# Loading one more half expert by whole rows, with smaller column slabs at the end

## The chip, the cores and the metric

The kernel runs on one core of a Trainium2 chip. The metric is the time of one execution on the device in microseconds (us), the median of several runs. A profile's span, from the program's first to its last instruction, is some 1.8 us shorter than that time (176.1 us in the profiled run of the kernel before, whose time was 177.85).

## The reference

Attention with a sliding or dilated window over 8 x 8 heads of 576 tokens makes 4608 token rows of 512. A soft mixture of experts then works on them: 8 experts, 4 slots each.

```python
logits = x @ phi                                   # 4608 x 32
slot_input = softmax_over_tokens(logits).T @ x     # 32 slots, 4 for each expert
for e in range(8):
    h = np.maximum(slot_input[e] @ w1[e], 0.0)     # w1: 8 x 512 x 1024 float32
    slot_out[e] = h @ w2[e]                        # w2: 8 x 1024 x 512 float32
return softmax_over_slots(logits) @ slot_out       # 4608 x 512 float32 out
```

w1 and w2 are 2 MB each for an expert, 32 MB in all, and the output is 9.44 MB.

## The kernel before

The loads go through GpSimd's DMA queue, which converts float32 to bf16 on the way (half an expert, 1 MB of float32, lands as 512 KB in the issue table); only phi and one piece of w1 come through SyncE's queue. The order of the loads is fixed. Attention's inputs and w1 come first, then w2 expert by expert. Experts 0 to 5 are loaded by whole rows. Experts 6 and 7 come last and are cut into two column halves, the "slabs": columns 0 to 255 of both, then columns 256 to 511 of both. When the first slab is there, the first half of the output's columns can be computed and stored while the second slab is still loading.

```python
def w2_piece(e, c0=0, n=8):          # whole rows
    ... moe_w2[e].rearrange("(p c) f -> p (c f)", c=8)[:, c0 * DM:(c0 + n) * DM]
    return (fn, n << 18, f"w2_{e}{c0}", b_w2[e] if e < 5 else [b_w5h[c0 // 4]])

def w2_slab(e, s, c0=0, n=8):        # 256 columns of each row: runs of 1 KB
    ... moe_w2[e].rearrange("(p c) f -> p c f", c=8)[:, c0:c0 + n, 256 * s:256 * s + 256]

wq += [w2_piece(e) for e in range(5)] + [w2_piece(5, 0, 4), w2_piece(5, 4, 4)]
for s in range(2):
    wq += [w2_slab(6, s), w2_slab(7, s, 0, 4), w2_slab(7, s, 4, 2),
           w2_slab(7, s, 6, 1), w2_slab(7, s, 7, 1)]
# ...
l2((0, 1, 2, 3), 0, 0, 512)          # L857: matmuls of the second layer, whole width
l2((4,), 0, 0, 512)
for y in range(2):
    l2((5,), 0, 0, 512, range(4 * y, 4 * y + 4), [b_w5h[y]])
# L872, L875: ScalarE and VectorE empty this accumulator
for x in (1, 2):                     # the two column halves
    l2((6,), x, 256 * x - 256, 256, bufs=[b_w2[6][x - 1]])
    for y, cs in enumerate((range(4), range(4, 6), range(6, 7), range(7, 8))):
        l2((7,), x, 256 * x - 256, 256, cs, [b_w2h[y][x - 1]])
    # L881: VectorE adds this half to the sum
# ... L901 output matmul, L910/L913 its eviction, L922 store
NA = 2.5                             # groups of 512 tokens stored in two column halves
```

With NA = 2.5 there are five first-half stores of 256 KB, five second-half stores of 256 KB, and then whole-width stores. A small list scheduler fixes each engine's order of instructions when the program is built.

The softmax here doesn't subtract the row's maximum and nothing guards it: scores larger than these inputs give would overflow.

Of the kernel before, what the change touches and what calls it, by code (L numbers as in the profile page):

```python
# [54 lines left out]
class Sched:  # L55
# [8 lines left out]
    def op(self, eng, fn, dur, prio, reads=(), writes=(), rmw=(), after=(), banks=(), name="",  # L64
           kind="c", nbytes=0, rate=422e3, lag=0.0, sem=None, tail=False):
        o = Op()
        o.eng, o.fn, o.dur, o.prio, o.name = eng, fn, dur, prio, name
        o.kind, o.bytes, o.rate, o.lag, o.sem, o.tail = kind, nbytes, rate, lag, sem, tail
        o.deps, o.succ = set(), []
        o.banks, o.opens, o.ord = [], [], None  # L70
        o.seq = len(self.ops)
        for a in after:
            if a is not None:
                o.deps.add(a)
        for b in reads:
            o.deps.update(b.w)
            b.r.append(o)
        for b in writes:
            if b.r:
                b.prev = b.w + b.r  # L80
                b.w, b.r = [], []
            o.deps.update(b.prev)
            b.w.append(o)
        for b in rmw:
            o.deps.update(b.prev)
            o.deps.update(b.w)
            o.deps.update(b.r)
            b.w.append(o)
        for b in list(reads) + list(writes) + list(rmw) + list(banks):
            if isinstance(b, Bank) and b not in o.banks:  # L90
                o.banks.append(b)
                if b.left == 0:
                    o.opens.append(b)
                b.left += 1
        o.deps.discard(o)
        self.ops.append(o)
        return o
# [99 lines left out]
def bass_dilated_sliding_attn__then__soft_moe_slots_kernel(  # L197
# [60 lines left out]
    def a(off, dims, p0=0, pn=128):  # L258
        return AP(ar, p0 * NBF + off, [[NBF, pn]] + dims)
# [4 lines left out]
    def af(off, dims, p0=0, pn=128):  # L264
        return AP(ar_f.tensor, (p0 * NBF + off) // 2, [[NBF // 2, pn]] + dims)
# [4 lines left out]
    def pf(bank, off, dims, p0=0, pn=128):  # L270
        return AP(ps, p0 * 4096 + bank * 512 + off, [[4096, pn]] + dims)
# [10 lines left out]
    def pet(n, cols):  # L282
        return (40.0 + n * max(cols / 2.4, 27.0)) * PE_SLOW / 1000.0
# [4 lines left out]
    def dvet(n, psum=False):  # L288
        return ((120 if psum else 58) + n) / 960.0
# [16 lines left out]
    b_w1 = [Buf(f"w1{e}") for e in range(8)]  # L306
    b_w2 = [[Buf(f"w2{e}{s}") for s in range(2)] for e in range(8)]
    b_sx = Buf("sx")
    b_w5h = [Buf(f"w5h{x}") for x in range(2)]
    b_w2h = [[Buf(f"w2h{x}{s}") for s in range(2)] for x in range(4)]  # L310
    b_htz, b_rt, b_so = Buf("htz"), Buf("rt"), [Buf("soA"), Buf("soB")]
    b_hsb = [Buf(f"hsb{x}") for x in range(2)]
# [1 line left out]
    def w2off(e):  # L314
        return o_w2 + e * 8 * DM if e < 5 else o_stg + (e - 5) * 8 * DM
# [25 lines left out]
    wq = []  # L341
# [15 lines left out]
    def w1_piece(e, r0=0):  # L357
        def fn():
            return pool.dma_start(a(o_w1 + e * 4096 + 1024 * r0, [[1, 4096 - 1024 * r0]]),
                                  w1_rows(e)[:, 1024 * r0:])  # L360
        return (fn, (4 - r0) << 19, f"w1_{e}", [b_w1[e]])

    def w2_piece(e, c0=0, n=8):
        def fn():
            return pool.dma_start(
                a(w2off(e) + c0 * DM, [[1, n * DM]]),
                moe_w2[e].rearrange("(p c) f -> p (c f)", c=8)[:, c0 * DM:(c0 + n) * DM])
        return (fn, n << 18, f"w2_{e}{c0}", b_w2[e] if e < 5 else [b_w5h[c0 // 4]])

    def w2_slab(e, s, c0=0, n=8):  # L370
        def fn():
            return pool.dma_start(  # L372
                a(w2off(e) + 256 * s + c0 * DM, [[DM, n], [1, 256]]),
                moe_w2[e].rearrange("(p c) f -> p c f", c=8)[:, c0:c0 + n, 256 * s:256 * s + 256])
        return (fn, n << 17, f"w2s_{e}{s}{c0}", [b_w2[e][s] if n == 8 else b_w2h[(0, 4, 6, 7).index(c0)][s]])

    wq += [w1_piece(e, 2 if e == 0 else 0) for e in range(8)]
    wq += [w2_piece(e) for e in range(5)] + [w2_piece(5, 0, 4), w2_piece(5, 4, 4)]
    for s in range(2):
        wq += [w2_slab(6, s), w2_slab(7, s, 0, 4), w2_slab(7, s, 4, 2),  # L380
               w2_slab(7, s, 6, 1), w2_slab(7, s, 7, 1)]
    nw = [0]

# [467 lines left out]
    def l2(es, x, col, n, cs=range(8), bufs=None):  # L851
        def fn():
            last = None
            for c in cs:
                for e in es:
                    g, j = e // 4, e % 4
                    last = pe.matmul(pf(sobank[x].idx, 0, [[1, n]], 32 * j, 32),  # L857
                                     a(o_htz + 1024 * g + 128 * c + 32 * j, [[1, 32]]),
                                     a(w2off(e) + DM * c + col, [[1, n]]),
                                     start=(c == 0 and (g == 0 or x > 0)),  # L860
                                     stop=(c == 7 and (x > 0 or e in (2, 3, 4, 5))))
            return last

        op(PE, fn, pet(len(cs), n * .92), T1 + 5 + 2 * es[0] + (20 if x == 2 else 0) + cs[0] / 8,
           reads=[b_htz] + (bufs or [b_w2[e][y] for e in es for y in range(2)]),
           rmw=[sobank[x]], name=f"L2{es[0]}{x}{cs[0]}")

    l2((0, 1, 2, 3), 0, 0, 512)
    l2((4,), 0, 0, 512)
    for y in range(2):  # L870
        l2((5,), 0, 0, 512, range(4 * y, 4 * y + 4), [b_w5h[y]])
    op(ACT, lambda: act.activation(a(o_so, [[1, 512]], 0, 64), pf(sobank[0].idx, 0, [[1, 512]], 0, 64),  # L872
                                   ACTF.Copy), actt(512), T1 + 10, reads=[sobank[0]], writes=b_so,
       name="SOx")
    op(DVE, lambda: dve.tensor_copy(af(o_sx, [[1, 512]], 64, 64), pf(sobank[0].idx, 0, [[1, 512]], 64, 64)),  # L875
       dvet(512, True), T1 + 10, reads=[sobank[0]], writes=[b_sx, b_p[2]], name="SOy")
    for x in (1, 2):
        l2((6,), x, 256 * x - 256, 256, bufs=[b_w2[6][x - 1]])
        for y, cs in enumerate((range(4), range(4, 6), range(6, 7), range(7, 8))):
            l2((7,), x, 256 * x - 256, 256, cs, [b_w2h[y][x - 1]])  # L880
        op(DVE, lambda x=x: dve.tensor_tensor(  # L881
            a(o_so + 256 * x - 256, [[1, 256]], 64, 64), pf(sobank[x].idx, 0, [[1, 256]], 64, 64),
            af(o_sx + 512 * x - 512, [[1, 256]], 64, 64), AluOp.add), dvet(256, True),
           T1 + 10 + 20 * x, reads=[sobank[x], b_sx], writes=[b_so[x - 1]], name=f"SO{x - 1}")
# [69 lines left out]
    for o in order:  # L954
        c = o.sem if o.kind == "dma" else ctr[o.eng]
# [4 lines left out]
        for d in o.deps:  # L960
            if d.eng == o.eng == PE:
                continue
            s, val = d.ev
# [60 lines left out]
```

## Time and profile before

| | before |
|---|---|
| median of 3 runs | 177.89 us |
| span of the profile | 176.1 us |
| MB written by DMA | 41.26 |
| last weight piece landed | 152.19 us into the span |
| first output store issued | 148.57 us |
| last store landed | 175.61 us |

Landings are read from the trace's record of DMA completions. From the last weight landing to the last store's landing is 23.42 us; I call it the tail. The prediction shows the lines of this profile.

In these lines PE is TensorE and PEld its weight loads, DVE is VectorE, ACT is ScalarE, POOL is GpSimd, and SP is SyncE, which issues the stores. `ar` and `ps` are the program's names for on-chip data and for accumulators, and L857 is line 857 of the kernel. A line of the windows table gives a stretch of time and its length, the busy time and number of instructions of PE, PEld, DVE, ACT and POOL, the granted TensorE clock as a share of full speed, the DMA share, and the GB/s written. The DMA share is the time of all packets over the time of 16 engines. Here it passes 1 (1.45 with the slabs), so the times of some packets overlap.

### The profile page before, as it was taken

What the parts mean: (1) busy time and instruction counts of PE and PEld (TensorE: products, weight loads), DVE (VectorE), ACT (ScalarE), POOL (GpSimd) and SP (SyncE); (2) the same over time, 40 slices, a digit from 0 to 9 for tenths busy, and PEclk for the clock granted to TensorE, in tenths of its full rate; (3) what the DMA queues carried; (4) which work ended last, traced back from release to release, by engine and by line L of the source; (5) the groups of instructions that cost most, each with busy time, mean ns of one, the idle gap of its engine ahead of it and who ended that gap; (6) DMA issues with size and microseconds to landing.
All of it is one profiled execution on the core that took longest, in us unless ns stands there. A gap on an engine that the chain in (4) does not pass through costs nothing.

```text
span 176.1 us, 4787 instructions
## 1 busy us (share of the span) xinstructions
PE 129.5 (74%) x2102; PEld 86.8 (49%) x2102; DVE 120.5 (68%) x218; ACT 104.4 (59%) x165; POOL 44.9 (25%) x90
## 2 busy tenths in 40 slices
PE   0008786799698998999998989996779676797000
PEld 0005564567566776676777567765434334431000
DVE  6899395669998989989998999657220014399200
ACT  2404378568879969889889788884301113299000
POOL 7659622214142223311460000394000000000000
PEclk9999999789999999999999999999755999999955
DMA  5999999999999999999999999999999999999997
GB/s 186 233 210 210 224 201 210 227 201 209 220 210 208 219 214 208 214 217 205 216 215 204 209 216 221 220 212 216 216 220 203 204 195 196 296 312 415 422 419 318
DMA packets 17492, 41.26 MB, mean 234 GB/s; under 512 B 1728, under 2 KB 8384, under 8 KB 15040
## 3 DMA queue, kind: packets, MB, share of 16 engines
q0 software_dynamic: 13328, 30.41, 90.2%
q1 hardware_dynamic: 4144, 10.55, 15.7%
q8 instruction: 16, 0.26, 0.5%
q14 instruction: 4, 0.03, 0.0%
HBM read 61.93 MB, written 9.44 MB: 405 GB/s over the span
## 4 chain that ended last, share of the span: by engine, by line
DMA 32%; PE 23%; DVE 21%; ACT 10%; POOL 4%; issue 2%; POOLq 0%; DVEq 0%
DMA ar<-in_moe_w_dram 18%; DMA ar<-in_v_dram 14%; PE ps L509 6%; DVE ar L488 6%; DVE ar L913 6%; ACT ar L548 5%; POOL ar L372 3%; PE ps L603 3%; PE ps L570 3%; ACT ar L670 2%; PE ps L693 2%; DVE ar L614 2%; PE ps L516 2%; PE ps L526 2%; ACT ar L576 2%
## 5 line engine op out<-in xcount | busy, mean ns | idle before, releaser
L548 ACT ACTIVATE ar<-ps 128x1152 bf16<-128x1152 f32 (+1 forms) x32 | 38.0, 1186 | 22.8 <-PE ps L533 13.2
L488 DVE STREAM_TRANSPOSE ar<-ar 128x576 uint32<-128x576 uint32 x40 | 48.3, 1239 | 0.6 <-DMA ar<-in_k_dram 0.3
L509 PE MATMUL ps<-ar 128*128 128x320 bf16 (+1 forms) x128 | 23.8, 312 | 15.5 <-DVE ar L488 13.7
L614 DVE TENSOR_TENSOR ar<-ps,fs 96x768 bf16<-96x768 f32 (+1 forms) x32 | 26.3, 822 | 1.2
L576 ACT ACTIVATE ar<-ps 128x768 bf16<-128x768 bf16 x32 | 25.0, 812 | 1.1 <-PE ps L570 1.0
L509 PEld LDWEIGHTS ps<-ar 128*128 128x128 bf16 x128 | 10.8, 102 | 21.0 <-DVE ar L488 13.7
L603 PE MATMUL ps<-ar 128*128 128x65 bf16 x320 | 15.6, 199 | 4.2 <-ACT ar L548 4.2
L570 PE MATMUL ps<-ar 128*128 128x128 bf16 x192 | 15.9, 229 | 1.8 <-DVE ar L614 1.0
L603 PEld LDWEIGHTS ps<-ar 128*128 128x128 bf16 x320 | 12.8, 101 | 7.4 <-ACT ar L548 4.8
L910 ACT ACTIVATE ar<-ps,fs 128x512 f32<-128x512 f32 (+1 forms) x23 | 11.4, 638 | 7.6 <-PE ps L901 7.6
L335 POOL DMA_DIRECT2D ar<-in_k_dram x16 | 8.9, 553 | 27.5 <-DVE ar L488 26.7
L610 DVE RECIPROCAL fs<-ps 96x12 f32<-96x12 f32 (+1 forms) x32 | 6.6, 206 | 12.7 <-PE ps L603 12.2
L570 PEld LDWEIGHTS ps<-ar 128*128 128x128 bf16 x192 | 12.4, 118 | 2.9 <-DVE ar L614 1.2
L913 DVE TENSOR_SCALAR ar<-ps,fs 128x512 f32<-128x512 f32 (+1 forms) x23 | 12.7, 629 | 1.0 <-PE ps L901 1.0
L335 POOL DMA_DIRECT2D ar<-in_v_dram x16 | 8.8, 547 | 13.7 <-DVE ar L488 10.4
L857 PE MATMUL ps<-ar 128*32 128x512 bf16 (+1 forms) x80 | 9.6, 338 | 2.9 <-DMA ar<-in_moe_w_dram 1.4
L693 PE MATMUL ps<-ar 128*128 128x288 bf16 x64 | 10.2, 307 | 1.2 <-ACT ar L677 1.2
L335 POOL DMA_DIRECT2D ar<-in_q_dram x16 | 8.7, 545 | 8.8 <-DVE fs L610 5.3
L901 PE MATMUL ps<-ar 128*128 128x512 bf16 (+1 forms) x46 | 9.9, 340 | 1.3 <-DVE ar L881 1.0
L670 ACT ACTIVATE ar<-ps 128x576 bf16<-128x576 bf16 x16 | 9.7, 659 | 0.9 <-PE ps L654 0.7
L673 ACT ACTIVATE ar<-ps 128x1024 bf16<-128x1024 bf16 x8 | 8.2, 1030 | 2.5 <-PE ps L660 2.3
L494 DVE STREAM_TRANSPOSE ar<-ar 128x160 uint32<-128x160 uint32 (+1 forms) x32 | 9.5, 409 | 0.1
(75 smaller groups left out, 182.8 us busy)
## 6 DMA issues: line engine op xcount, KB each, us to landing
ar<-in_moe_w_dram POOLq DMA_DIRECT2D x12, 1024.0 KB, 25.9
out_dram<-ar SPq DMA_DIRECT2D x6, 1024.0 KB, 8.6
ar<-in_k_dram POOLq DMA_DIRECT2D x16, 288.0 KB, 21.1
ar<-in_q_dram POOLq DMA_DIRECT2D x16, 288.0 KB, 21.5
ar<-in_v_dram POOLq DMA_DIRECT2D x16, 288.0 KB, 20.5
ar<-in_moe_w_dram POOLq DMA_DIRECT2D x5, 512.0 KB, 28.1
out_dram<-ar SPq DMA_DIRECT2D x10, 256.0 KB, 3.8
ar<-in_moe_w_dram SPq DMA_DIRECT2D x1, 1024.0 KB, 5.1
```

Source lines behind the costliest of these rows:

```text
L335: return pool.dma_start(a(o_stg + (s * 3 + j) * 1152, [[1, 1152]]), src[b, 4 * dl:4 * dl + 4].rearrange("h (p t) d -> (h p) (t d)", p=32))
L488: return dve.transpose(au(o_dst, [[1, 18], [18, 32]]), au(src, [[32, 18], [1, 32]]))
L509: pe.matmul(pf(h, 0, [[1, W]]), a(o_id, [[1, 128]]), a(msk, [[1, W]]), start=True, stop=False)
L548: eo = op(ACT, lambda P=P, W=W: act.activation(a(P, [[W, 4], [1, W]]), AP(ps, 0, [[4096, 128], [512, 4], [1, W]]), ACTF.Exp, scale=SCALE), ...
L570: last = pe.transpose(pb(bank.idx, bb * 256 + par * 32, [[64, 4], [1, 32]]), src, a(o_id, [[1, 128]]))
L576: op(ACT, lambda t=t, bank=bank: act.activation(a(o_vb[vs] + 3 * t * VBK, [[66, 12], [2, 32], [1, 2]]), pb(bank.idx, 0, [[64, 12], [1, 32] ...
L603: last = pe.matmul(pf(bank.idx + x, 65 * t, [[1, 65]]), w, a(VB + t * VBK + 66 * h, [[1, 65]]), start=True, stop=True)
L614: op(DVE, lambda hp=hp, bank=bank: dve.tensor_tensor(a(ox + 128 * hp, [[64, 2], [256, NT], [1, 64]], 0, rows), pf(bank.idx, 0, [[512, 2], ...
L670: fn = lambda c=c + x, bank=bank: act.activation(a(o_xt[xt] + 576 * c, [[1, 576]]), pb(bank.idx, 0, [[1, 576]]), ACTF.Copy)
L693: last = pe.matmul(pf(bank.idx, 0, [[1, 288]]), a(o_phis + 128 * c, [[1, 128]]), a(o_xt[xt] + 576 * c + 288 * g, [[1, 288]]), start=(c == ...
L910: op(ACT, lambda: act.activation(dst, src(), ACTF.Copy, scale=sca), actt(cw, .1), prio + .1, reads=[bank, b_rinv], writes=wr, name=f"OE{G} ...
L913: op(DVE, lambda: dve.tensor_scalar(dst, src(), sca, None, op0=AluOp.mult), dvet(cw, True) + .08, prio + .1, reads=[bank, b_rinv], writes= ...
```

## The change

The intent is to move bytes out of the slow slabs and into fast whole rows (196 against 216 GB/s written in the profile before), without losing the overlap of the second slab with the first-half stores. Half of expert 6's rows are loaded whole and go into the whole-width accumulator. The slabs shrink from 4 MB to 3 MB in all, and expert 5 comes in one transfer.

```diff
-        return (fn, n << 18, f"w2_{e}{c0}", b_w2[e] if e < 5 else [b_w5h[c0 // 4]])
+        return (fn, n << 18, f"w2_{e}{c0}", b_w2[e] if e < 6 else [b_w6h])
...
-    wq += [w2_piece(e) for e in range(5)] + [w2_piece(5, 0, 4), w2_piece(5, 4, 4)]
+    wq += [w2_piece(e) for e in range(6)] + [w2_piece(6, 0, 4)]
     for s in range(2):
-        wq += [w2_slab(6, s), w2_slab(7, s, 0, 4), w2_slab(7, s, 4, 2),
+        wq += [w2_slab(6, s, 4, 4), w2_slab(7, s, 0, 4), w2_slab(7, s, 4, 2),
...
-    for y in range(2):
-        l2((5,), 0, 0, 512, range(4 * y, 4 * y + 4), [b_w5h[y]])
+    l2((5,), 0, 0, 512)
+    l2((6,), 0, 0, 512, range(4), [b_w6h])
...
-        l2((6,), x, 256 * x - 256, 256, bufs=[b_w2[6][x - 1]])
+        l2((6,), x, 256 * x - 256, 256, range(4, 8), [b_w2[6][x - 1]])
```

The rest of the diff renames buffers and sets the accumulators' start and stop flags.

More of the change, by code (lines that the diff above doesn't have):

```diff
@@ L308, in bass_dilated_sliding_attn__then__soft_moe_slots_kernel @@
     b_sx = Buf("sx")
-    b_w5h = [Buf(f"w5h{x}") for x in range(2)]
+    b_w6h = Buf("w6h")
     b_w2h = [[Buf(f"w2h{x}{s}") for s in range(2)] for x in range(4)]
@@ L374, in fn @@
                 moe_w2[e].rearrange("(p c) f -> p c f", c=8)[:, c0:c0 + n, 256 * s:256 * s + 256])
-        return (fn, n << 17, f"w2s_{e}{s}{c0}", [b_w2[e][s] if n == 8 else b_w2h[(0, 4, 6, 7).index(c0)][s]])
+        return (fn, n << 17, f"w2s_{e}{s}{c0}", [b_w2[e][s] if e == 6 else b_w2h[(0, 4, 6, 7).index(c0)][s]])
     wq += [w1_piece(e, 2 if e == 0 else 0) for e in range(8)]
-    wq += [w2_piece(e) for e in range(5)] + [w2_piece(5, 0, 4), w2_piece(5, 4, 4)]
+    wq += [w2_piece(e) for e in range(6)] + [w2_piece(6, 0, 4)]
     for s in range(2):
-        wq += [w2_slab(6, s), w2_slab(7, s, 0, 4), w2_slab(7, s, 4, 2),
+        wq += [w2_slab(6, s, 4, 4), w2_slab(7, s, 0, 4), w2_slab(7, s, 4, 2),
                w2_slab(7, s, 6, 1), w2_slab(7, s, 7, 1)]
@@ L859, in fn @@
                                      a(w2off(e) + DM * c + col, [[1, n]]),
-                                     start=(c == 0 and (g == 0 or x > 0)),
-                                     stop=(c == 7 and (x > 0 or e in (2, 3, 4, 5))))
+                                     start=(c == 0 and g == 0 or x > 0 and c == (4 if e == 6 else 0)),
+                                     stop=(c == (3 if e == 6 and x == 0 else 7) and (x > 0 or e in (3, 4, 5, 6))))
             return last
```

## The prediction

Two passages are cut from it, where marked: they told rules of the hardware that no trace of this case shows, and an estimate of the slab rate made from one of them. What is left of that paragraph is read from the trace. No term of the sum is cut. It came to -0.25 us, which is 1 MB at the measured 392 instead of 432 GB/s (2.67 against 2.43 us), and 177.89 - 0.25 = 177.64, rounded to 177.65 us.

> **What bounds the kernel now.** I read five views: the page's forty slices, the chain that ended last, the windows table, the issue table for two single transfers, and the timeline of the tail.
>
> The slices come first (each is 176.1 / 40 = 4.4 us; digits are tenths of busy time, GB/s are bytes written by the DMA engines).
>
> ```profile
> ## 2 busy tenths in 40 slices
> ...
> DMA  5999999999999999999999999999999999999997
> GB/s 186 233 210 210 224 201 210 227 201 209 220 210 208 219 214 208 214 217 205 216 215 204 209 216 221 220 212 216 216 220 203 204 195 196 296 312 415 422 419 318
> ```
>
> The DMA row is full nearly from end to end. The loads convert float32 to bf16, so 210 GB/s written is about 420 GB/s read. Slices 33 and 34 (195, 196) are the column slabs, the slowest loads; 35 and 36 (296, 312) are the change from loading to storing; the rest is storing. The chain (start us, length us, what) says the same.
>
> ```profile
> 120.13 32.05 DMA ar<-in_moe_w_dram
> 152.19 0.04 issue
> 152.23 0.30 PE ps L857
> ...
> 152.55 0.44 DVE ar L881
> ...
> 153.04 0.42 PE ps L901 x2
> ...
> 153.48 8.64 DVE ar L913 x15
> ```
>
> The last weight piece was issued at 120.1 and landed at 152.2, so it waited in a queue for 32 us. After it come a matmul, an addition and the first output tiles. The chain then walks through evictions on VectorE, but the last store was issued at about 164 and the run ends at 176.1: from 155 on the store queue is the bound.
>
> The rates, in the windows table (last column GB/s written, the one before it DMA share):
>
> ```profile
> 120.00:132.00 12.00, 8.19 (x73) 4.72 (x74) 4.28 (x13) 2.68 (x8) 0.72 (x2) 0.73 1.03 216
> ...
> 142.00:149.00 7.00, 5.09 (x34) 2.70 (x30) 2.07 (x5) 1.65 (x4) 0.00 (x0) 1.00 1.45 196
> ```
>
> Whole rows write at 216 GB/s (432 read), slabs at 196 (392 read). Two transfers of half an expert each (expert 5; 512 KB written, 1 MB read; the last number is us from issue to landing) confirm the first rate:
>
> ```profile
> ar<-in_moe_w_dram POOLq DMA_DIRECT2D x1, 512.0 KB, 26.2
> ```
>
> ```profile
> ar<-in_moe_w_dram POOLq DMA_DIRECT2D x1, 512.0 KB, 28.1
> ```
>
> They were issued at 112.8 and 113.3, so they landed at about 139.0 and 141.4, 2.4 us apart for 1 MB. TensorE takes each slab piece up as it lands, so its weight loads date the landings:
>
> ```profile
> 144.09 0.77 PEld L857 LDWEIGHTS ps<-ar 128*32 128x32 bf16 x8 [1.35 <-DMA ar<-in_moe_w_dram]
> ...
> 146.80 0.09 PEld L857 LDWEIGHTS ps<-ar 128*32 128x32 bf16 x1 [0.26 <-DMA ar<-in_moe_w_dram]
> ...
> 148.57 16.08 SPq L922 DMA_DIRECT2D out_dram<-ar  x17
> 149.50 0.77 PEld L857 LDWEIGHTS ps<-ar 128*32 128x32 bf16 x8 [0.80 <-DMA ar<-in_moe_w_dram]
> ...
> 152.23 0.09 PEld L857 LDWEIGHTS ps<-ar 128*32 128x32 bf16 x1 [0.31 <-DMA ar<-in_moe_w_dram]
> ```
>
> The first slab (2 MB read) took 146.80 - 141.4 = 5.4 us, the second 152.23 - 146.80 = 5.43 us: 2.7 us for 1 MB. Expert 6's piece alone, 1 MB, took 144.09 - 141.4 = 2.7.
>
> How loading passes into storing:
>
> ```profile
> 149.50:152.20 2.70, 2.30 (x15) 1.20 (x15) 0.61 (x2) 0.38 (x2) 0.00 (x0) 1.00 1.21 289
> 152.20:153.40 1.20, 0.65 (x5) 0.46 (x6) 0.43 (x1) 0.03 (x1) 0.00 (x0) 1.00 1.02 358
> 153.40:155.00 1.60, 1.60 (x13) 1.11 (x10) 1.52 (x4) 1.60 (x5) 0.00 (x0) 1.00 0.55 193
> 155.00:158.50 3.50, 3.39 (x14) 0.95 (x13) 3.50 (x7) 3.50 (x7) 0.00 (x0) 1.00 1.03 346
> ```
>
> From 153.4 to 155.0 only about half of the DMA engines work (share 0.55). I read it so: half of the engines got through their loads early, stored their part of the five first-half stores, and idle until the second-half stores come; the other half, loading until 152, are still at the first-half stores. Both meet at 155.0, and from there everything is full.
>
> [...] expert 5's halves landed 2.4 us apart, what their bytes need, so joining them should save nothing. [...] the second slab took 5.43 us, though stores were issued from 148.57 on, and the first, alone, 5.4.
>
> **The change part by part.**
>
> Expert 5 in one transfer: one issue less, and no byte or run shape that matters (4 KB written runs become 8 KB). Before 2 x 2.4 us, after 4.8. Its matmuls start at one landing instead of two, off the path. 0 us.
>
> Half of expert 6 whole: 1 MB read moves from slab rate to row rate. 1,048,576 B at 392 GB/s is 2.67 us, at 432 it is 2.43; from the landings 2.7 against 2.4. I take 0.25 us off. It lies straight on the load queue, which is the bound before 152.2, so it counts in full. The number of issues stays at 17, 20 us and more before their landings, so issue cost is hidden.
>
> Moved: landings become 141.4 (expert 5), 141.4 + 2.43 = 143.85 (expert 6, whole half), then each slab 1.5 MB, 5.42 x 3/4 = 4.07 us: 147.9 for the first, 152.0 for the second. So the first slab is complete 1.1 us later than now (146.8), and the last piece 0.25 earlier. First-half outputs move 1.1 us later: first store at about 149.7 instead of 148.57. Expert 6's four extra row matmuls run at 143.9, and the two copies that empty the first accumulator (now 143.27, 0.59 and 0.69 us) move behind them, to some 145.5 to 146; they are needed at 147.9, so 2 us to spare. Matmul work shrinks by four half-width instructions (276 ns each), hidden.
>
> After the last landing, nothing changes in kind: 1.85 us from there to the first second-half store (issued at 154.0 by the view of the store line, landed 2.3 us later), then the same 9.44 MB of stores. The engines that finish loads at about 152 find five stores queued in both kernels, whose 1.31 MB takes them to 155. Both ends of the meeting at 155.0 shift by the same 0.25. Sum: -0.25 us, and 177.89 - 0.25 = 177.64, rounded to **177.65 us**.
>
> **The rivals.**
>
> (A) The idle half of the engines is filled. First-half stores come 1.1 us later, so less idle remains in 153.4 to 155.0; that idle is worth 1.6 x (1 - 0.55/1.03) = 0.75 us of the whole set. If the engines that lag handed work on, the end would come up to 0.75 us earlier still: 176.9. Against it: the stores after 155.0 depend on the last landing, 0.25 earlier only, and the lagging half has no idle time to give. I think the fill moves the idle time ahead, to before the later first stores. 7%.
>
> (B) A new gap. Stores come too late for the lagging engines. They need the first at about 151.8; it is issued at 149.7, and takes under 1 us to start (148.57 issued, stores flow in 149.5:152.2). That leaves about 1.2 us. If TensorE's fixed order put the first-half tiles behind expert 6's second slab piece (about 149.2) they would lose some 0.6 us, still inside. Only if they came behind the whole second slab would about 1.5 to 2 us be lost: 179.4. 3%.
>
> (C) The transfer is hidden anyway: rates drift, or the lagging engines lag by another amount (the spread of the 16 is some 2 us, by the half-busy stretch), so that 0.25 us drowns: 177.9 to 178.1, the range of three runs before being 177.81 to 178.1. 12%.
>
> **Range and chances.** The mechanism gives 0.2 to 0.3 us; run-to-run scatter is 0.3, A pulls down and C up. That makes 177.3 to 178.0. Two per cent is 3.6 us: faster would need a gain larger than the idle time plus the saving (1.0 us), slower needs more than B's worst case. So 0.005 faster, 0.985 within, 0.01 slower.
>
> **What would show it right or wrong.** Right: the last weight landing at 151.9 to 152.0 and the stretch from it to the end unchanged at 23.9 us; the last piece of the first slab at about 147.9, the first store at 149.7; slab stretches still at 195 GB/s, each near 4.1 us. A shows as a stretch from last landing to end shorter by over 0.3 us. B shows as a stretch in which all engines fall idle between 152 and 155. The saving's size fails if the whole half of expert 6 takes more than 2.5 us, or if slabs of 1.5 MB need over 4.2 us. I would be wrong outright if the order of tail instructions changed so that output tiles wait for the second slab.

## The result, and the profile after

The changed kernel took 177.65 us (median of 6 runs, 177.49 to 177.88), the kernel before in the same rounds 177.97 us (6 runs, 177.81 to 178.12). The ratio is 0.9982, with a 95% interval of 0.9969 to 0.9995.

The profiled run was the slowest of the six, 177.88 us, and its span is the 176.1 us of the profile before. The gain must therefore be read from the stage that was changed. The page's DMA line counts packets; first the kernel before, then the changed one:

```profile
DMA packets 17492, 41.26 MB, mean 234 GB/s; under 512 B 1728, under 2 KB 8384, under 8 KB 15040
```

```profile
DMA packets 16468, 41.26 MB, mean 234 GB/s; under 512 B 1728, under 2 KB 7360, under 8 KB 13888
```

The bytes are the same; 1024 of the small packets are gone. The windows table of the changed kernel (the columns are as in the prediction) has the two load rates and the change from loading to storing:

```profile
120.00:132.00 12.00, 8.19 (x66) 4.92 (x67) 4.71 (x13) 3.12 (x8) 0.89 (x2) 0.67 1.03 216
142.00:149.00 7.00, 5.32 (x41) 2.29 (x33) 1.12 (x2) 0.59 (x1) 0.00 (x0) 1.00 1.41 194
...
149.50:152.20 2.70, 2.48 (x18) 1.24 (x15) 1.89 (x5) 1.66 (x5) 0.00 (x0) 1.00 0.95 218
152.20:153.40 1.20, 0.65 (x5) 0.46 (x6) 0.43 (x1) 0.03 (x1) 0.00 (x0) 1.00 1.06 358
153.40:155.00 1.60, 1.60 (x13) 1.12 (x10) 1.52 (x4) 1.60 (x5) 0.00 (x0) 1.00 0.88 303
155.00:158.50 3.50, 3.39 (x14) 0.96 (x13) 3.50 (x7) 3.50 (x7) 0.00 (x0) 1.00 1.03 344
```

The row rate is as before (216). The second line mixes two rates in the changed kernel, whose whole half of expert 6 landed at 143.99 us. By landings that half took 2.46 us and the two slabs of 1.5 MB took 4.05 and 4.14 us, some 2.7 us for 1 MB as before. In the passage, 149.5 to 152.2 fell from 289 to 218 GB/s, which is 71 x 2.7 = 0.19 MB not written there. 153.4 to 155.0 rose from 193 to 303 GB/s, 110 x 1.6 = 0.18 MB. The idle time moved from behind the first-half stores to ahead of them, and nothing was gained or lost by that. The timeline of the changed kernel's tail (weight loads of TensorE, and the store queue):

```profile
148.08 0.09 PEld L857 LDWEIGHTS ps<-ar 128*32 128x32 bf16 x1 [0.25 <-DMA ar<-in_moe_w_dram]
...
149.85 14.78 SPq L922 DMA_DIRECT2D out_dram<-ar  x17
...
152.22 0.09 PEld L857 LDWEIGHTS ps<-ar 128*32 128x32 bf16 x1 [0.34 <-DMA ar<-in_moe_w_dram]
```

The first slab was complete 1.28 us later than before (148.08 against 146.80), the first store was issued 1.28 us later (149.85 against 148.57), and the last piece landed at the same time. The chain that ended last has the same links as before:

```profile
120.24 31.95 DMA ar<-in_moe_w_dram
152.18 0.04 issue
152.23 0.30 PE ps L857
```

That the last landing did not move (152.19 and 152.18) has its cause before the changed stage. Expert 4's w2, the last transfer that is the same in both kernels, landed at 136.53 us before and at 136.70 in this profile. From there to the last landing it is 15.66 us before and 15.48 after: the changed stage is 0.18 us shorter, and in this profile the attention stage happened to take that back. Over all fourteen profiles it landed between 136.40 and 136.78, so chance moves it by more than the whole gain.

### The profile page after: what moved, and what is told of

Its sections match the earlier page's. It is cut to its first block, busy times and chain, and to the rows that moved or that the text cites. A ratio compares the mean times of both kernels' runs of the same rounds, so it can differ in the third digit from the quotient of the medians.

```text
span 176.1 us, 4779 instructions
## 1 busy us (share of the span) xinstructions
PE 128.2 (73%) x2098; PEld 85.7 (49%) x2098; DVE 121.2 (69%) x218; ACT 104.4 (59%) x165; POOL 44.5 (25%) x90
## 4 chain that ended last, share of the span: by engine, by line
DMA 46%; DVE 21%; PE 15%; ACT 4%; POOL 4%; issue 2%; POOLq 0%; DVEq 0%
DMA ar<-in_q_dram 28%; DMA ar<-in_moe_w_dram 18%; DVE ar L913 6%; DVE ar L488 5%; PE ps L509 4%; POOL ar L372 3%; DVE ar L614 2%; PE ps L570 2%; ACT ar L548 2%; ACT ar L670 2%; DVE ar L494 2%; PE ps L693 2%; DVE ar L444 2%; PE ps L516 2%; PE ps L603 1%
## 5 line engine op out<-in xcount | busy, mean ns | idle before, releaser
L509 PE MATMUL ps<-ar 128*128 128x320 bf16 (+1 forms) x128 | 23.0, 303 | 17.9 <-DVE ar L488 13.7
L509 PEld LDWEIGHTS ps<-ar 128*128 128x128 bf16 x128 | 10.5, 99 | 22.8 <-DVE ar L488 13.7
L603 PE MATMUL ps<-ar 128*128 128x65 bf16 x320 | 15.0, 195 | 3.9 <-ACT ar L548 3.9
L603 PEld LDWEIGHTS ps<-ar 128*128 128x128 bf16 x320 | 12.4, 99 | 6.9 <-ACT ar L548 4.5
L570 PEld LDWEIGHTS ps<-ar 128*128 128x128 bf16 x192 | 12.4, 118 | 2.9 <-DVE ar L614 1.2
L693 PE MATMUL ps<-ar 128*128 128x288 bf16 x64 | 11.1, 326 | 1.2 <-ACT ar L677 1.2
L857 PE MATMUL ps<-ar 128*32 128x512 bf16 (+1 forms) x76 | 9.0, 347 | 1.9 <-DMA ar<-in_moe_w_dram 1.2
## 6 DMA issues: line engine op xcount, KB each, us to landing
ar<-in_q_dram POOLq DMA_DIRECT2D x16, 288.0 KB, 23.4
```

Of the source, the lines that this page charges most:

```text
L509: pe.matmul(pf(h, 0, [[1, W]]), a(o_id, [[1, 128]]), a(msk, [[1, W]]), start=True, stop=False)
L570: last = pe.transpose(pb(bank.idx, bb * 256 + par * 32, [[64, 4], [1, 32]]), src, a(o_id, [[1, 128]]))
L603: last = pe.matmul(pf(bank.idx + x, 65 * t, [[1, 65]]), w, a(VB + t * VBK + 66 * h, [[1, 65]]), start=True, stop=True)
L693: last = pe.matmul(pf(bank.idx, 0, [[1, 288]]), a(o_phis + 128 * c, [[1, 128]]), a(o_xt[xt] + 576 * c + 288 * g, [[1, 288]]), start=(c == ...
```

## The experiments

My theory: 1 MB of reads leaves the slab rate, the load queue gets 0.25 us shorter, and the tail stays as it is. The rivals: joining expert 5's transfers matters, filling the idle DMA engines matters, the gain is chance. All outputs were correct. The table has every profile; "1 KB MB" is the MB read in runs of 1 KB, "stretch" is from expert 4's landing to the last weight landing, "lead" is how long before the last landing the first store was issued, "tail" is as defined above, and "median" is the time. Profile times are from the one profiled run, all in us.

| run | 1 KB MB | stretch | last landing | first store | lead | tail | median |
|---|---|---|---|---|---|---|---|
| before | 4 | 15.66 | 152.19 | 148.57 | 3.62 | 23.42 | 177.97 |
| changed | 3 | 15.48 | 152.18 | 149.85 | 2.33 | 23.45 | 177.65 |
| e1_again | 3 | 15.42 | 152.07 | 149.83 | 2.24 | 23.43 | 177.75 |
| e10_again | 3 | 15.44 | 151.91 | 149.65 | 2.26 | 23.46 | 177.61 |
| e2_join5 | 4 | 15.62 | 152.27 | 148.75 | 3.52 | 23.39 | 177.79 |
| e3_half6 | 3 | 15.47 | 151.97 | 149.80 | 2.17 | 23.43 | 177.68 |
| e5_cols5 | 5 | 15.85 | 152.54 | 150.32 | 2.22 | 23.42 | 178.17 |
| e9_slab125 | 2.5 | 15.31 | 151.84 | 150.46 | 1.38 | 24.04 | 178.29 |
| e4_slab1 | 2 | 15.16 | 151.90 | 151.13 | 0.77 | 24.65 | 179.71 |
| e11_slab1 | 2 | 15.11 | 151.64 | 151.86 | -0.22 | 25.61 | 179.73 |
| e6_slabhalf | 1 | 14.90 | 151.30 | 151.93 | -0.63 | 26.04 | 180.08 |
| e12_late | 3 | 15.42 | 152.00 | 150.84 | 1.16 | 24.32 | 178.60 |
| e7_na2 | 3 | 15.44 | 152.04 | 149.98 | 2.06 | 23.79 | 178.07 |
| e8_na3 | 3 | 15.43 | 152.21 | 149.94 | 2.27 | 23.45 | 177.88 |

**The changed kernel again, twice.** No edit.

> The changed kernel once more, with more rounds. Load-rate theory (1 MB read moves from 392 to 432 GB/s, on the path in full): 0.25 us less than the kernel before, ratio 0.9986. Rival 'hidden': ratio 0.9995 to 1.0005, the first 0.32 us having been chance. Rival 'idle half of the DMA engines is filled': 0.5 us less or more, ratio 0.997 or lower.

> The changed kernel a third time, to settle the size of the gain: ratio to before between 0.9982 and 0.9992 if 0.2 to 0.3 us are gained, 0.9995 to 1.0005 if nothing is. Stretch from expert 4's landing to the last landing 15.4 to 15.5 us (before 15.66), tail 23.4 us, in either case.

Measured: e1 177.75 us (6 runs, one of them 178.4) against 177.86 before (11 runs), ratio 0.9995 (0.998 to 1.001). e10 177.61 us (5 runs) against 177.78 (9 runs), ratio 0.999 (0.9977 to 1.0002). With the first result and e3 below, all four ratios are under 1, and two of the four intervals (e1's and e10's) contain 1; e1's ratio lies at the edge of what was written down for 'hidden'. From end times alone the gain is 0.1 to 0.3 us and no more exact. The stretch is steadier: 15.42 to 15.48 us in the seven profiles with 3 MB of slabs (mean 15.44), 15.62 and 15.66 with 4 MB (mean 15.64): 0.20 us.

**Expert 5 joined, and nothing else.** On the kernel before:

```diff
-    wq += [w2_piece(e) for e in range(5)] + [w2_piece(5, 0, 4), w2_piece(5, 4, 4)]
+    wq += [w2_piece(e) for e in range(6)]
-    for y in range(2):
-        l2((5,), 0, 0, 512, range(4 * y, 4 * y + 4), [b_w5h[y]])
+    l2((5,), 0, 0, 512)
```

> The kernel before, with only expert 5's two half transfers joined into one; slabs stay at 4 MB. Load-rate theory: no byte changes its run length, so 0.0 us, ratio 0.9995 to 1.0005, and the stretch from expert 4's landing to the last landing unchanged at 15.66 us. Rival 'a fixed cost for each transfer is saved': 0.1 to 0.3 us less.

Measured: 177.79 against 177.86 us, ratio 0.9993 (0.9981 to 1.0005), stretch 15.62 against 15.66. Joining saves nothing that these runs can see. The end times alone would allow up to 0.34 us; in the stage itself the difference is 0.04.

**Half of expert 6 whole, and expert 5 still in halves.** On the changed kernel:

```diff
-    wq += [w2_piece(e) for e in range(6)] + [w2_piece(6, 0, 4)]
+    wq += [w2_piece(e) for e in range(5)] + [w2_piece(5, 0, 4), w2_piece(5, 4, 4), w2_piece(6, 0, 4)]
```

> The changed kernel with expert 5 still in two halves: the half of expert 6 loaded whole and slabs of 3 MB are all that is left of the change. Load-rate theory: the whole gain is here, 0.25 us less than before, ratio 0.9986, equal to the changed kernel within 0.1 us. Rival 'joining counts': ratio 0.9995 or more.

Measured: 177.68 us (5 runs) against 177.86, ratio 0.9986 (0.9974 to 0.9998), stretch 15.47. The whole effect is in this part.

**Expert 5 in two column halves.** On the changed kernel; the bytes, the matmuls and their order stay.

```diff
-    wq += [w2_piece(e) for e in range(6)] + [w2_piece(6, 0, 4)]
+    wq += [w2_piece(e) for e in range(5)] + [w2_slab(5, 0), w2_slab(5, 1), w2_piece(6, 0, 4)]
```

> The changed kernel, with expert 5 read in two column halves (1 KB runs) in place of whole rows; its matmuls wait for both, and nothing else differs, the order of the other instructions included. Load-rate theory: 2 MB move from 432 to 392 GB/s, 0.5 us more than the changed kernel, 0.25 more than the kernel before, ratio to before 1.0014. Rival 'the gain came from the later first-half stores, not from the load rate': as the changed kernel, ratio 0.9982 to 0.9986.

Measured: 178.17 us against 177.86 before, ratio 1.0016 (1.0002 to 1.003), as expected. The stretch grew from 15.44 to 15.85, 0.41 us for 2 MB. By landings the two halves of expert 5 took 2.62 and 2.66 us, where e1's rows took 4.85 for both. The windows table does not show this: from 137.5 to 141.5 it has 209 GB/s in e5 and 202 in e1, as the 16 parts of a load land up to 3.0 us apart (in the changed kernel's profile 2.88 to 3.00 in this stage) and so fall into different windows. The first store came just as far ahead of the last landing (2.22 us), and the tail was 23.42. So it is the run length that costs (1 KB read, 512 B written; no run separates the two), about 0.20 us for 1 MB, and not where the slabs stand or when stores begin.

**All of expert 6 whole: slabs of 1 MB, twice.** On the changed kernel; the additions shrink to expert 7's rows.

```diff
-    wq += [w2_piece(e) for e in range(6)] + [w2_piece(6, 0, 4)]
+    wq += [w2_piece(e) for e in range(7)]
-        wq += [w2_slab(6, s, 4, 4), w2_slab(7, s, 0, 4), w2_slab(7, s, 4, 2),
+        wq += [w2_slab(7, s, 0, 4), w2_slab(7, s, 4, 2),
```

> One step further: all of expert 6 whole, slabs of expert 7 alone (2 MB in all, 1 MB each). Load rate alone gives 0.50 us less than before (last landing 0.5 us earlier). But the first slab is then complete only 2.7 us before the last load, first store issued near 150.8, flowing near 151.7, while the lagging DMA engines have no load left from 151.3: 0.4 us of new idle time. Theory with that gap: 0.1 us less than before, ratio 0.9994, and 0.15 slower than the changed kernel. Rival 'only the load rate counts': ratio 0.9972. Rival 'filling the idle half of the engines counts': 0.997 or lower.

Measured: 179.71 us (6 runs, 178.81 to 179.97), ratio 1.0086 (1.0064 to 1.0108). My expectation missed by 2 us of the median. The loads did as told, the stretch being 0.5 us below that of before. The tail grew by 1.23 us in the profiled run. The windows table shows the gap:

```profile
151.50:152.20 0.70, 0.70 (x8) 0.54 (x6) 0.70 (x3) 0.70 (x3) 0.00 (x0) 1.00 0.19 65
152.20:153.40 1.20, 0.46 (x5) 0.28 (x4) 0.84 (x3) 0.18 (x1) 0.00 (x0) 1.00 1.04 342
153.40:155.00 1.60, 1.60 (x13) 1.20 (x11) 1.43 (x4) 1.54 (x5) 0.00 (x0) 1.00 1.03 341
```

From 151.5 to 152.2 the DMA engines are nearly idle (share 0.19). I had foreseen that gap. I had not foreseen that nothing is stored ahead of it: all stores then run on all engines at once, at 341 GB/s. The profiled run was of the lower of two levels, so I took one more.

> The 1 MB slabs again, whose times had two levels (178.8 twice, 179.6 to 180.0 four times) and whose profile showed the lower. If this profile is of the upper level: the further 1 us lies between the last landing and the last store (tail 25.6 us in place of 24.65), if the stores' own rate is what varies, or before the last landing (its time 1 us later), if the loads vary.

Measured: this profile was of the upper level (179.53 us), and the tail was 25.61 as the first of the two possibilities has it. But the reason given there was wrong, and the number that I hit was luck: the stores' rate did not vary, the first store was issued 0.73 us later than in e4 although the last landing came earlier. The windows table of e4, then of e11, just before and during the matmuls of expert 6 (the third number from the end is the granted TensorE clock):

```profile
143.70:146.50 2.80, 0.00 (x0) 0.00 (x0) 0.00 (x0) 0.00 (x0) 0.00 (x0) 1.00 1.21 186
146.50:149.50 3.00, 2.83 (x16) 1.22 (x16) 0.70 (x1) 0.59 (x1) 0.00 (x0) 1.00 1.34 179
```

```profile
143.70:146.30 2.60, 0.70 (x3) 0.03 (x2) 0.00 (x0) 0.00 (x0) 0.00 (x0) 0.50 1.22 188
146.30:149.50 3.20, 3.15 (x16) 1.52 (x16) 0.01 (x1) 0.02 (x1) 0.00 (x0) 0.59 1.33 178
```

In e11 the clock stood at 0.50 before and 0.59 during these matmuls, in e4 at 1.00. From the first of them to the emptying of the accumulator it was 3.21 us in e11 (146.27 to 149.48) and 1.94 in e4 (146.53 to 148.47), so it began to be emptied 1.01 us later. TensorE idled just before these matmuls in both, 1.90 us in e11 and 2.98 in e4. Why the granted clock was lower in one of two profiles of the same program, they do not show. One profile of each level is all there is; that the clock makes the two levels is not shown for the other runs, which were not profiled.

**Slabs of 0.5 MB.** As e4, and half of expert 7 whole:

```diff
-    wq += [w2_piece(e) for e in range(7)]
+    wq += [w2_piece(e) for e in range(7)] + [w2_piece(7, 0, 4)]
-        wq += [w2_slab(7, s, 0, 4), w2_slab(7, s, 4, 2),
+        wq += [w2_slab(7, s, 4, 2),
```

> Experts 5, 6 and the first half of 7 whole, slabs of 0.5 MB each (1 MB in all). Load rate alone: last landing 0.75 us earlier than before, ratio 0.9958. With the gap: first slab complete at about 150.0, first store issued at 151.9 or later and flowing at 152.8, while no engine has a load left from 151.1: 1.6 us of idle DMA or more, so 0.9 to 1.5 us slower than before, ratio 1.005 to 1.008.

Measured: 180.08 us against 177.86, ratio 1.0125 (1.0108 to 1.0141), worse than expected. The stretch is 0.76 us shorter than before, as expected; the tail is 2.62 us longer.

**Slabs of 1.25 MB.** On the changed kernel, three quarters of expert 6 whole:

```diff
-    wq += [w2_piece(e) for e in range(6)] + [w2_piece(6, 0, 4)]
+    wq += [w2_piece(e) for e in range(6)] + [w2_piece(6, 0, 6)]
-        wq += [w2_slab(6, s, 4, 4), w2_slab(7, s, 0, 4), w2_slab(7, s, 4, 2),
+        wq += [w2_slab(6, s, 6, 2), w2_slab(7, s, 0, 4), w2_slab(7, s, 4, 2),
```

> Half a step further than the changed kernel: three quarters of expert 6 whole, slabs of 1.25 MB each (2.5 MB in all). From the runs so far: 0.24 us for each MB taken out of slabs, so the stretch from expert 4's landing to the last landing 15.3 us (changed kernel 15.42 to 15.48). The first store is issued near 150.4 and flows near 151.3, just before the lagging engines end their loads at about 151.4, so no gap yet: tail from last landing to last store 23.4 us, 0.1 us faster than the changed kernel. Rival 'the edge is already passed' (as with 1 MB slabs): tail 23.8 us or more, 0.3 us slower or more.

Measured: 178.29 us against 177.78, ratio 1.0025 (1.0012 to 1.0039). The stretch was 15.31 as expected, the tail 24.04 and not 23.4. The edge is already passed half a step after the changed kernel.

**The first-half stores later, the loads untouched.** On the changed kernel, the output matmuls depend on expert 6's matmuls of the second slab:

```diff
-        l2((6,), x, 256 * x - 256, 256, range(4, 8), [b_w2[6][x - 1]])
+        late = l2((6,), x, 256 * x - 256, 256, range(4, 8), [b_w2[6][x - 1]])
...
-           pet(1, cw), prio, reads=[b_et] + rd, writes=[bank], name=f"O{G}{j}{c0}")
+           pet(1, cw), prio, reads=[b_et] + rd, writes=[bank], after=[late], name=f"O{G}{j}{c0}")
```

> The changed kernel with the same loads, but the first output tiles placed behind expert 6's matmuls of the second slab on TensorE: only the first-half stores come later, by about 1.0 us. From the profiles so far the tail (last landing to last store) is 23.43 us as long as the first store is issued at least 2.0 us before the last landing, and grows one for one below that (1.38 us ahead: 24.03; 0.77: 24.65; 0.22 after it: 25.61; 0.63 after: 26.04). Here 1.1 to 1.3 us ahead, so a tail of 24.1 to 24.3 and a time 0.7 us above the changed kernel, ratio to before 1.0025 to 1.003, with the last landing unmoved. Rival 'the 1 MB and 1.25 MB slabs lose by something of the loads or of the smaller matmul groups': tail 23.4, time as the changed kernel.

Measured: 178.60 us against 177.87, ratio 1.0041 (1.0028 to 1.0055). The time is a little above what I expected (1.0025 to 1.003), and so is the tail, 24.32 against 24.1 to 24.3. The stretch is 15.42, as in the changed kernel. The store queue's line in the timeline and the windows table:

```profile
150.84 6.55 SPq L922 DMA_DIRECT2D out_dram<-ar  x10
```

```profile
149.50:152.20 2.70, 2.70 (x22) 1.88 (x20) 1.87 (x5) 1.94 (x5) 0.00 (x0) 1.00 0.66 117
152.20:153.40 1.20, 0.68 (x7) 0.49 (x6) 0.64 (x3) 0.14 (x1) 0.00 (x0) 1.00 1.02 344
153.40:155.00 1.60, 1.60 (x12) 1.00 (x9) 1.60 (x5) 1.60 (x5) 0.00 (x0) 1.00 1.02 339
```

The first store was issued 0.99 us later than in the changed kernel. From 149.5 to 152.2 the engines wrote 117 GB/s in place of 218, 0.27 MB less. There is no idle time left from 152.2 on to do it in: 339 against 303 GB/s from 153.4 to 155.0 gives back 0.06 MB, 344 against 358 before that loses 0.02. The rest, 0.23 MB at some 343 GB/s, is an estimated 0.7 us; the tail grew by 0.87 us. So lateness of the first stores alone makes the loss, with all else as in the changed kernel.

The completions of the stores show how time is lost with no engine idle. In the kernel before, the engines that lag (the last seven of the 16 completions) go from one first-half store to the next in 0.67 to 0.69 us in the mean, those in front (the first seven) in 0.74 to 0.76. A lagging engine therefore catches up: the spread of the 16 falls from 2.36 us at the first of the five stores to 2.02 at the last. In e12 all start together, and all take 0.74 to 0.80 (256 KB at its 339 to 344 GB/s is 0.76 to 0.77). Why a lagging engine is faster, no run shows.

The five profiles with a long tail and five first-half stores lie on one line: tail = 23.43 + (1.98 - lead), wherever the lead is under 1.98. I drew it through the first four before e12 ran, with the corner put down as 2.0. For e9 it gives 24.03 (measured 24.04), for e4 24.64 (24.65), for e11 25.63 (25.61), for e6 26.04 (26.04), for e12 24.25 (24.32). From 2.17 up the tail is flat; between 1.38 and 2.17 there is no profile with five such stores, so the corner at 1.98 is where the two lines meet. The changed kernel leads by 2.24 to 2.33 us (e3, with the same slabs, by 2.17), so 0.2 to 0.35 us are to spare; the kernel before had 1.6.

**Four or six first-half stores in place of five.** On the changed kernel:

```diff
-    NA = 2.5
+    NA = 2        # e7; 3 in e8
-    for G, x in [(2, 2)] + [(G, x) for G in range(3, 9) for x in (0, 2)]:
+    for G, x in [(G, x) for G in range(2, 9) for x in (0, 2)]:    # from 3 in e8
```

> The changed kernel with four first-half stores in place of five (two groups of 512 tokens, not two and a half). Queue theory: the lagging engines run out of stores 0.6 us before the second-half stores flow, at the price of 0.6 us, less 0.2 us because half a group is stored in 2 KB runs (2.5 us for 1 MB) and not in two pieces of 1 KB runs: 0.3 to 0.4 us slower than the changed kernel, ratio to before 1.0002 to 1.0005. Rival 'the end follows the last load alone and has slack there': 0.2 us faster than the changed kernel, ratio 0.997.

> The changed kernel with six first-half stores (three groups). Queue theory: no engine is idle in either, half a group goes in 1 KB runs at 0.69 + 0.76 us in place of 1.25: 0.2 us slower than the changed kernel, ratio to before 0.9994. Rival 'idle engines still cost time there' (share 0.88 in the stretch 153.4 to 155.0, worth 0.25 us): as fast as the changed kernel or faster, ratio 0.998 or lower.

Measured: e7 178.07 us against 177.86 before, ratio 1.0018 (1.0006 to 1.0031). The ratio is above what I wrote. The changed kernel did not run in these rounds; by the kernel before (0.3 us faster in the mean) and the gain of 0.1 to 0.3 us, the loss against it is some 0.4 to 0.6 us. The profile fits the 0.3 to 0.4 us expected: its tail is 0.36 us longer than the usual 23.43, and the windows table shows why:

```profile
153.40:155.00 1.60, 1.54 (x11) 0.97 (x9) 1.60 (x5) 1.60 (x5) 0.00 (x0) 1.00 0.59 205
```

The engines run dry before the second-half stores come (share 0.59). e8 took 177.88 us, ratio 0.9996 (0.9984 to 1.0009). Its engines have no idle time there:

```profile
153.40:155.00 1.60, 1.44 (x12) 1.14 (x11) 1.49 (x4) 1.60 (x5) 0.00 (x0) 1.00 1.04 354
```

Still its tail is that of the changed kernel (23.45). The completions show that a gain and a loss cancel. The tenth store of 256 KB was complete 6.91 us after the last weights, in the changed kernel's three profiles 7.10 to 7.16: filling the idle time won 0.2 us. The next 512 KB took 1.53 us in two pieces of 1 KB runs, in the changed kernel 1.31 to 1.35 us in one whole-width store: the 0.2 us that I expected it to lose. (e7's expectation says 2 KB runs for whole-width stores; the changed kernel's trace has packets of 4 KB in this one and of 8 KB in those of 1 MB.) So the rival of this expectation was right too, about the idle time. No experiment clearly beat the changed kernel.

## Why the prediction was right

The median of 177.65 us is the predicted number to the hundredth, and that is luck: the repeats gave 177.75 and 177.61, the gain by end times was 0.1 to 0.3 us, and the changed stage is 0.20 us shorter, not 0.25. What was right is the mechanism.

**The bound** was read rightly. The load queue sets the last landing and the stores set what follows: the tail is 23.39 to 23.46 us in all eight profiles whose first store leads by 2.1 us or more.

**Expert 5 joined: 0 us.** Shown by e2 and, from the other side, by e3.

**Half of expert 6: 0.25 us, in full.** The mechanism is right, the size a little too large. The stretch shrank by 0.20 us, and e5 gives 0.41 us for 2 MB back, 0.20 for one. Over all sizes from 5 MB to 1 MB it is (15.85 - 14.90) / 4 = 0.24 us for each MB, with single steps of 1 MB from 0.20 to 0.31. The prediction's own limits held: the whole half of expert 6 took 2.46 us (at most 2.5), the slabs 4.05 and 4.14 (at most 4.2). The quoted "2.7 against 2.4" rounded in favour of the larger number. Why the shorter runs are slower, no run shows.

**What moved.** First slab at 147.9 and first store at 149.7 were measured at 148.04 and 149.85 in a profile that entered the stage 0.18 us late, and at 147.85 and 149.65 in e10; the last landing, 152.0, at 151.91 to 152.18.

**Rival A** (idle engines filled) fell as argued: in the changed kernel the idle time moved and the tail stayed. But idle time of half of the engines is not worthless: e8 fills it with a sixth store, wins 0.2 us and loses them again to that store's shorter runs.

**Rival B** was rightly given little chance, but its working was wrong: "That leaves about 1.2 us" and a loss of 0.6 us being "still inside". e12 delays the first store by 0.99 us and loses 0.87 us of tail. What is to spare is 0.2 to 0.35 us. The step counted only when the lagging engines need a store. It left out that the early engines must by then have stored their share: if they have not, all sixteen store at once at some 340 GB/s, the lagging engines have nothing to catch up with, and time is lost with no engine idle. The expectation for e4 failed by the same step.

**Rival C** (the gain drowns in scatter) is half true: single runs overlap, and e1's and e10's intervals contain 1. But none of the three medians of the changed kernel lies in its 177.9 to 178.1.

## What to carry to other kernels

Where a DMA queue was the bound here, the value of a changed transfer was its own time in that queue (0.20 us for 1 MB, by the stretch): compare rates of long and short runs in the trace, and date landings from the last transfer that is equal in both kernels, since earlier chance can hide a gain of 0.1% (expert 4's landing moved between 136.40 and 136.78 us). Cutting a load into a late part whose wait is covered by other traffic had an edge here: the tail stayed at 23.4 us with the first store issued 2.1 us or more before the last load landed, and from a lead of about 2.0 us down each us later cost one (tails of 24.04 to 26.04 us at leads of 1.38 to -0.63). Look for that edge before shrinking the late part further. And weigh a gain against its price in the same profile: e8's equal tail hid a gain and a loss of 0.2 us each.

## Other measurements of these runs

- On the engines that landed last, the stores were not seen to slow the loads: the second slab of the kernel before took 5.43 us, though store packets ran from 149.49 us on, through its last 2.7 us; the first took 5.4 us alone. The trace has no engine number for a packet, so this is read from the landings.
- In the kernel before, the 16 completions of one load spread over 0.76 us at the first load and over 2.60 us at the last, with about half of them (8) some 2 us behind. The trace does not say which engines these are, nor why. They catch up in the stores that follow (0.67 to 0.69 us for a part of a 256 KB store against 0.74 to 0.76).
- The stores wrote 339 to 358 GB/s with 1 KB runs on all engines, and 419 to 420 GB/s in the whole-width stores, whose packets are of 8 KB (4 KB in the one of 512 KB).
- What the lower clock (0.59 in the matmuls of expert 6) cost e11 is not the slower matmuls alone: at a matmul group that opens the stores it set the first store back by 0.73 us, to 0.22 us after the last landing, and the times of the kernel with 1 MB slabs lie on two levels 0.7 to 1.2 us apart (178.8 against 179.5 to 180.0), of which one run each was profiled.
